# Value products by 64x64 quarters and 32-row tiles, and the second batch's attention turned by VectorE and moved, in a pooled-attention and sine-MLP kernel

## The chip, the cores and the metric

One core of one Trainium2 chip. The metric is device time in microseconds (us), of single executions; smaller is better. A result says "ratio" for the mean time of one kernel's fast runs over the mean time of the kernel before in the same rounds on the same chip, so it is not quite the ratio of the medians that stand beside it. In profile lines PE is TensorE (PEld its weight loads), DVE VectorE, ACT ScalarE, POOL GpSimd, and SPq and ACTq are the DMA issues of SyncE and ScalarE. The granted clock is the share of the full TensorE clock that the throttle let through; "half clock" means stretches where that share is 0.5. A call of the value products leaves two records in a trace (16 for a batch's eight).

## The reference

```python
# q, k, v: (8, 8, 576, 64) float32; w_in (512, 2048), w_out (2048, 512), alpha (2048)
k_p = k.reshape(B, H, 72, 8, D).mean(axis=3)          # 576 keys pooled to 72
v_p = v.reshape(B, H, 72, 8, D).mean(axis=3)
scores = scale * q @ k_p.T                            # (576 x 72) per head
attn = softmax(scores)
x = (attn @ v_p).transpose(0, 2, 1, 3).reshape(4608, 512)
h = x @ w_in
s = np.sin(alpha * h)
out = (h + s * s / (alpha + 1e-9)) @ w_out
```

## The kernel before

TensorE computes both large products with a seven-product scheme: L580 is one line of the hidden product (records of 128x128 against 256 columns), L874 the output product. A batch's attention is spread over the 28 slots of the hidden product of the batch before; a slot is eight L580 records, 1.76 us. Each slot first runs what the slot before left over (`left0` to `left6`: evictions, sines, squares, sums), then the extras that `carry` gives it, then its product. So every engine's order is the program's order.

For a batch from the third on, softmax runs with queries on partitions; VectorE turns the result in 32x32 blocks into a scratch tile `tr`, and twelve DMAs on SyncE's queue move the blocks of each 32-row group onto the right partitions of `aT`. Then 16 records of value products follow, and 16 small ones for the last 64 queries.

```python
def turn(i):
    n = rows[i]
    if i == 0:
        self.tr = self.new_tr().rearrange("p (c h t i) -> p c h t i", c=3, h=H, i=32)
    nc.vector.transpose(out=self.tr[:n, :, :, i, :].rearrange("p c h i -> p h c i"),        # L347
                        in_=ex[:n, i].rearrange("p h (c i) -> p h c i", i=32))

def move(part):
    for a in (2 * part, 2 * part + 1):
        w = 160 if a < 2 else 128
        for c in range(3):
            m = min(32, Sp - 32 * c)
            flat = lambda x: x.rearrange("k h t i -> k h (t i)")[:, :, 0:w]
            nc.sync.dma_start(out=flat(aT[0][32 * c:32 * c + m, a]),                        # L356
                              in_=flat(self.tr[32 * a:32 * a + m, c]))

def values(hp):
    vp = self.vp[b]
    ps = ... else self.abank([P, 4 * P])              # one of three banks in turn
    for e in range(2):
        h = 2 * hp + e
        x = ... aT[0][:, :, h, 0:4, :] ...
        nc.tensor.matmul(ps[64 * e:64 * e + 64, :], vp[:, h, :], x, start=True, stop=True)  # L382
    to_x(ps.rearrange("p (t j) -> p j t", t=4), hp, 0, 512)     # ScalarE evicts, L371

def turn_q(self, b, part):        # the next-but-one batch's q, the same way, through the same scratch
    if part == 0:
        self.tr = self.new_tr()
    # ... part 0, 1: nc.vector.transpose (L162); part 2, 3: sixteen moves (L169)

# carry(u), batches from the third on (cut)
at((12, 12, 13, 14, 14)[i], A.turn, i)
at(14, A.move, 0)
at(15, A.move, 1)
for hp in range(4):
    at((0, 1, 3, 4)[hp], self.load_kv, "v", b, hp)
    if b < last:
        at((12, 13, 14, 17)[hp], self.load_kv, "k", b + 1, hp)   # L109; GpSimd sums them, L114
    at(24, A.values, hp)
at(24, A.values_rest)                                            # L392
at(26, self.att[b + 1].k_t)                                      # TensorE turns the next keys, L194
# turn_q of batch u + 2 at slots 21 to 24
```

The second batch is different: TensorE turns its q (L205) and its attention (L263) itself, ScalarE and VectorE evict, and nothing is moved.

## Time and profile before

| | before |
|---|---|
| median of the first three runs | 952.11 us (950.91 to 952.22) |
| span of the profiled run | 942.5 us, mean granted clock 0.995 |
| TensorE stops over 0.15 us in that span | 16.5 us, 15.5 of them before 95 us |
| first score product of batch three | 111.1 us |
| from there, block to block | 57.5, 58.0, 57.5, 57.5, 57.7 us |
| last block's start to the end | 543.3 us |

How to read it: I use the first score product of each batch as a mile post, because from the third batch on all blocks do the same.

### The profile page before, as it was taken

To read this page: it belongs to the slowest core of one execution; us is meant where nothing else is said; L and a number is where in the kernel's file an instruction comes from. 1 tells how busy PE (TensorE), PEld (TensorE's weight loads), DVE (VectorE), ACT (ScalarE), POOL (GpSimd) and SP (SyncE) were. 2 spreads that over 40 slices of the span, in tenths; PEclk is the share of its full clock that TensorE was granted. 3 is DMA by queue.
4 is the path that set the end of the run, shared out by engine and by line. 5 is a ranking of instruction groups with operands and counts; after the bars stand their busy time and mean duration, and the time that the engine had idled before them with its cause. 6 is when DMAs were issued, how large, how long until landed. Compare 5 with 4: busy or idle time off the path is not lost.

```text
span 942.5 us, 17456 instructions
## 1 busy us (share of the span) xinstructions
PE 920.3 (98%) x6853; PEld 820.5 (87%) x6853; DVE 686.6 (73%) x1025; ACT 441.0 (47%) x1005; POOL 200.4 (21%) x220
## 2 busy tenths in 40 slices
PE   7898999999999999999999999999999999999997
PEld 5576787887878878787888899999999999999997
DVE  6477584766748677485356889988979888979795
ACT  4647576585766758677696651211111111111111
POOL 4337264452634536250000000000000000000000
PEclk9989999999999999999999999999999999999999
DMA  9375456666476663744624545353434444343501
GB/s 249 91 229 154 122 190 154 213 153 201 155 195 190 169 196 97 191 150 135 233 90 136 194 140 146 107 163 90 147 106 129 124 122 131 112 141 90 162 14 38
DMA packets 139841, 137.82 MB, mean 146 GB/s; under 512 B 49088, under 2 KB 108240, under 8 KB 139760
## 3 DMA queue, kind: packets, MB, share of 16 engines
q1 hardware_dynamic: 138688, 135.53, 49.5%
q10 hardware_dynamic: 1072, 1.19, 0.4%
q8 instruction: 54, 0.88, 0.4%
q14 instruction: 27, 0.22, 0.1%
HBM read 74.46 MB, written 47.19 MB: 129 GB/s over the span
## 4 chain that ended last, share of the span: by engine, by line
PE 89%; DVE 3%; DMA 2%; ACT 1%; SPq 1%; POOL 1%; issue 1%; DVEq 0%; ACTq 0%; POOLq 0%
PE PS L580 42%; PE PS L874 40%; PE PS L382 3%; PE PS L224 2%; DMA g_bridge<-h 1%; SPq L356 1%; DMA home<-in_k_dram 1%; ACT s L593 1%; DVE h L559 1%; DMA a<-in_moe_w_in_dram 0%; DVE as L446 0%; DVE tr L347 0%; DVE sm L253 0%; POOL home L121 0%; PE PS L339 0%
## 5 line engine op out<-in xcount | busy, mean ns | idle before, releaser
L580 PE MATMUL PS<-home,a 128*128 128x256 f32 x1152 | 268.2, 384 | 5.5 <-DVE h L559 4.9
L580 PEld LDWEIGHTS PS<-home,a 128*128 128x128 f32 x1152 | 215.9, 191 | 40.0 <-DVE h L559 7.2
L580 PE MATMUL PS<-home,as 128*128 128x256 f32 x864 | 202.4, 382 | 0.3 <-ACT PS L606 0.2
L580 PEld LDWEIGHTS PS<-home,as 128*128 128x128 f32 x864 | 161.3, 190 | 25.1 <-ACT PS L606 3.1
L114 POOL TENSOR_TENSOR kvin<-kvin 72x512 f32<-72x512 f32 x112 | 120.0, 1072 | 159.2 <-DMA kvin<-in_v_dram 103.8
L874 PE MATMUL PS<-s,wb 128*128 128x144 f32 x896 | 119.4, 286 | 0.4 <-ACT PS L987 0.4
L874 PEld LDWEIGHTS PS<-s,wb 128*128 128x128 f32 x896 | 113.7, 190 | 0.7 <-ACT PS L987 0.6
L593 ACT ACTIVATE s<-s,c 128x256 f32<-128x256 f32 (+1 forms) x216 | 110.0, 572 | 0.0
L586 ACT ACTIVATE s<-h,al 128x256 f32<-128x256 f32 x144 | 65.3, 501 | 83.1 <-DVE h L559 83.1
L559 DVE TENSOR_TENSOR h<-PS,p 128x512 f32<-128x512 f32 x72 | 49.2, 683 | 61.2 <-ACT s L593 26.0
L987 ACT COPY PS<-PS 128x144 f32<-128x144 f32 x56 | 14.7, 263 | 145.7 <-PE PS L874 144.3
L586 ACT ACTIVATE s<-PS,al 128x256 f32<-128x256 f32 x144 | 60.0, 467 | 34.9 <-PE PS L580 19.2
L874 PE MATMUL PS<-r,wb 128*128 128x144 f32 x512 | 73.2, 286 | 0.0
L874 PE MATMUL PS<-s,a 128*128 128x144 f32 x512 | 73.2, 286 | 0.0
L874 PEld LDWEIGHTS PS<-r,wb 128*128 128x128 f32 x512 | 67.1, 190 | 0.1
L874 PEld LDWEIGHTS PS<-s,a 128*128 128x128 f32 x512 | 67.1, 190 | 0.0
L647 DVE TENSOR_TENSOR h<-PS,s 128x512 f32<-128x512 f32 x36 | 24.6, 684 | 49.1 <-ACT s L593 48.4
L1006 ACT COPY PS<-PS 128x144 f32<-128x144 f32 x56 | 14.7, 263 | 88.5 <-PE PS L874 88.5
L874 PE MATMUL PS<-s,we 128*128 128x144 f32 x384 | 54.9, 286 | 0.0
L874 PE MATMUL PS<-x,wb 128*128 128x144 f32 x384 | 54.9, 286 | 0.0
L246 POOL TENSOR_TENSOR ex<-ex,sm 128x576 f32<-128x576 f32 (+1 forms) x36 | 40.4, 1147 | 53.2 <-ACT PS L618 21.5
L874 PEld LDWEIGHTS PS<-s,we 128*128 128x128 f32 x384 | 50.4, 190 | 0.1
(146 smaller groups left out, 1218.5 us busy)
## 6 DMA issues: line engine op xcount, KB each, us to landing
g_bridge<-h SPq DMA_DIRECT2D x72, 512.0 KB
r<-g_bridge SPq DMA_DIRECT2D x31, 1152.0 KB
out_dram<-o SPq DMA_DIRECT2D x128, 72.0 KB
kvin<-in_k_dram SPq DMA_DIRECT2D x28, 288.0 KB
kvin<-in_v_dram SPq DMA_DIRECT2D x28, 288.0 KB
q<-in_q_dram SPq DMA_DIRECT2D x7, 1024.0 KB
a<-in_moe_w_in_dram SPq DMA_DIRECT2D x16, 256.0 KB
q<-tr SPq DMA_DIRECT2D x48, 80.0 KB
```

The lines of the kernel that those rows point to most:

```text
L114: (eng or nc.gpsimd).tensor_tensor(out=o, in0=t[:, :, 0:w], in1=t[:, :, w:2 * w], op=OP.add)
L224: nc.tensor.matmul(ps[e][r:r + q.shape[-1], hp, :], q[s], k, start=True, stop=True)
L246: eng.tensor_tensor(out=E(n, i, 0, H), in0=E(n, i, 0, H), in1=sm[:n].unsqueeze(2).to_broadcast([n, H, Sp]), op=OP.mult)
L382: nc.tensor.matmul(ps[64 * e:64 * e + 64, :], vp[:, h, :], x, start=True, stop=True)
L559: add = lambda o, x, y: nc.vector.tensor_tensor(out=o, in0=x, in1=y, op=OP.add)
L580: nc.tensor.matmul(ps[:, jj, :], self.A[p][:, kk, f * P:(f + 1) * P], x[:, kk, :], start=(start and jj == 0 and kk == 0), stop=(kk == 1), ...
L586: nc.scalar.activation(out=G.s[:, i, jj, j, :], in_=src[:, jj], func=AF.Sin, scale=self.al[:, f:f + 1])
L593: nc.scalar.activation(out=x, in_=x, func=AF.Square, scale=self.c[:, f:f + 1])
L647: add = lambda o, x, y: self.nc.vector.tensor_tensor(out=o, in0=x, in1=y, op=OP.add)
L874: nc.tensor.matmul(out, W[:, J // 2, J % 2, :], A[:, J, :], start=(start and J == 0), stop=(J == self.NJ - 1), skip_group_check=True)
L987: nc.scalar.copy(out=x1[:, 0, :], in_=x0[:, 1, :])
L1006: nc.scalar.copy(out=x1[:, 1, :], in_=x1[:, 0, :])
```

## The change

The intent: the value products of 72 keys run in two lanes of 72x64 only. Cut into 64 keys and 8 keys, the 64-key part runs in four 64x64 quarters, and the last eight keys of four heads are put together in one 32-row tile (masked to its heads), so that four of them run side by side. Besides, the second batch is turned by VectorE and moved by DMA like the others, which takes those turnings off TensorE.

```diff
-            aT.append(self.ap.tile([Sp, 4, H, 5, 32], F32, name="aT"))
+            self.aM = self.ap.tile([P, 4, 4, 5, 32], F32, name="aM")     # 64 keys of two heads, one above the other
+            self.aR = self.ap.tile([P, 4, 5, 32], F32, name="aR")        # last 8 keys of four heads, four copies of 32 rows
         def move(part):
-            for a in (2 * part, 2 * part + 1):
-                for c in range(3): ...                                   # 12 moves
+            def heads(a):
+                for s in range(2):
+                    for c in range(2):
+                        r = 64 * s + 32 * c
+                        nc.sync.dma_start(out=flat(self.aM[r:r + 32, a], a), in_=flat(tr[32 * a:32 * a + 32, c, s], a))
+            if part == 0:
+                for a in range(4):
+                    for s in range(2):
+                        nc.sync.dma_start(out=flat(self.aR[32 * s:32 * s + 32, a], a), in_=flat(z[32 * a:32 * a + 32, s], a))
+                heads(0)
+            else:
+                heads(1)
+                for a in range(0, 4, 2):                                 # copies of the rest onto the other rows
+                    x = self.aR[:, a:a + 2, 0:4].rearrange("p a t i -> p a (t i)")
+                    nc.sync.dma_start(out=x[64:], in_=x[:64])
+                heads(2)
+                heads(3)                                                 # 26 moves in all
-        def values(hp): ...
+        def values(hps, banks):
+            for o, (main, _) in zip(ps, parts):
+                for e, (w, x) in enumerate(main):                        # 64x64 quarters, L451
+                    nc.tensor.matmul(o[64 * e:64 * e + 64], w, x, start=True, stop=False, skip_group_check=True)
+            for o, (_, (w, x)) in zip(ps, parts):                        # 32-row tiles, L453
+                nc.tensor.matmul(o, w.rearrange("p e d -> p (e d)"), x, start=False, stop=True, skip_group_check=True)
+            for hp, o in zip(hps, ps):
+                to_x(...)
# carry, steady batches
-            at(15, A.move, 1)
+            at(14, A.move, 1)
-                    at((12, 13, 14, 17)[hp], self.load_kv, "k", b + 1, hp)
-                at(24, A.values, hp)
-            at(24, A.values_rest)
+                    at((12, 13, 15, 18)[i], self.load_k, b + 1, i)
+            at(25, lambda: A.values((0, 2, 1, 3), A.free_banks()))
+            at(26, lambda: A.values_rest((5, (self.turn + 1) % 5)))
# ... second batch: pairs_q, q_t and a_t go; turn_q(1) at slot 2, turn at 17 to 19, move at 19 and 20, values at 25
# ... first batch: laid out for quarters; second weight block and second batch's keys loaded earlier
```

## The prediction

> **What bounds the kernel now.** I read the page's first lines, then the chain that ended last, then TensorE's groups kept apart by shape, and last the timeline of one steady attention batch. The page and its chain:
>
> ```profile
> PE 920.3 (98%) x6853; PEld 820.5 (87%) x6853; DVE 686.6 (73%) x1025; ACT 441.0 (47%) x1005; POOL 200.4 (21%) x220
> PE 89%; DVE 3%; DMA 2%; ACT 1%; SPq 1%; POOL 1%; issue 1%; DVEq 0%; ACTq 0%; POOLq 0%
> ```
>
> TensorE is busy 98% and carries 89% of the chain, so matmul time removed is time gained, provided no wait takes its place. Only about 15 us of TensorE are idle, nearly all before 95 us (window table: 6.43 us in 40 to 50). The longest stop there:
>
> ```profile
> 47.56 0.83 DVE L446 TENSOR_TENSOR as<-a,a 128x512 f32<-128x512 f32 x1 [6.35 <-DMA a<-in_moe_w_in_dram]
> 49.05 3.45 PE L580 MATMUL PS<-home,a 128*128 128x256 f32 x8 [3.80 <-DVE h L559]
> ```
>
> VectorE waits 6.35 us for a weight block queued late, TensorE waits for VectorE. What the change touches on TensorE:
>
> ```profile
> L382 PE MATMUL PS<-aT,vp 72*64 72x512 f32 x128 | 29.7, 600 | 0.6 <-DMA aT<-tr 0.5
> L224 PE MATMUL PS<-kblk,q 64*64 64x72 f32 x912 | 21.2, 229 | 0.0
> L392 PE MATMUL PS<-aT,vp 72*64 72x64 f32 x128 | 5.2, 222 | 0.0
> L263 PE MATMUL PS<-ident,ex 128*72 128x128 f32 x32 | 4.2, 274 | 1.9 <-ACT aT L268 1.9
> L205 PE MATMUL PS<-ident,q 128*128 128x128 f32 x16 | 2.6, 283 | 2.6 <-ACT aT L266 2.6
> ```
>
> The value products (L382, L392) are 35 us over eight batches. L263 and L205 are turnings on TensorE, mostly of the second batch. Now a steady batch: chain, DMA queue and VectorE:
>
> ```profile
> 239.39 31.60 PE PS L580 x144
> 270.99 3.58 PE PS L382 x16
> 274.57 0.46 PE PS L392 x16
> ```
>
> ```profile
> 257.93 3.87 SPq L356 DMA_DIRECT2D aT<-tr  x6
> 261.91 0.60 SPq L109 DMA_DIRECT2D kvin<-in_k_dram  x1
> 262.56 4.15 SPq L356 DMA_DIRECT2D aT<-tr  x6
> ```
>
> ```profile
> 270.31 3.02 DVE L162 STREAM_TRANSPOSE tr<-q 128x1024 f32<-128x1024 f32 x4 [4.91 <-DMA g_bridge<-h]
> 273.26 0.64 DVE L647 TENSOR_TENSOR h<-PS,s 128x512 f32<-128x512 f32 x1
> 273.84 1.20 DVE L647 TENSOR_TENSOR h<-h,s 128x1024 f32<-128x1024 f32 x1
> ```
>
> This is the point of the case. Twelve moves of the turned attention matrix (L356) are issued back to back, 8.0 us for twelve, 0.67 us each with gaps. The semaphores show the first landing 2.5 us after its issue, the last at 270.14. Value products start at 270.99: **the slack is 0.8 us**. VectorE's next turning of q (L162) reuses the same scratch tile, so it waits for the same landing, and everything behind it on VectorE waits too.
>
> **What the Trainium skill says.** "TensorEngine Tiling (Array Packing)", Key Properties: different tiles load and multiply in parallel, and changing the tiling mode drains TensorE. The trace agrees: 32 records of L224 in four quarters take 0.66 us; a slot of eight L580 records takes 1.92 us after such a switch, against 31.60/18 = 1.76 in a row, so a return costs 0.17 us. "DMA: Bandwidth & Descriptors", Rules for kernel authors: many small transfers should be merged, under 64 KB one pays mostly overhead. The trace agrees: 40 KB and 160 KB moves both hold the queue 0.53 to 0.74 us. "TensorE: Matmul & The Clock Gate", What's actually happening: a free-running window of about 3.4 us without work halves the clock. The trace agrees: after the 3.80 us stop above, eight records took 3.45 us instead of 1.9. The same page, under the array's architecture, calls VectorE and ScalarE strict FIFO; L647 behind L162 shows it.
>
> **The change part by part.**
>
> Value products, batches 2 to 8. Before: 16 records of 512 columns in two lanes, 3.58 us. Eight rows of 439 ns (two passes of 512 columns at the 2.33 columns/ns of 256x2/219 ns) make 3.51, so the two lanes are full. After: main part, 16 records in four lanes, 4 x 0.44 = 1.76 us; the last eight keys, 8 records in four lanes, 2 x 0.44 = 0.88. Together 2.64, a saving of 0.9. Against it one more switch between tilings (0.1 to 0.2), 24 records instead of 16 in the rest (0.46 becomes about 0.55), and one more return because the rest moves to the next slot (0.17). **Net about -0.3 to -0.5 us a batch, some -3 us in all.** That is the intent, and it is small.
>
> First two batches on TensorE: q turnings (L205) -3.1, attention turnings (L263) -5.2, value sums in two column lanes (3.9 + 1.2 become about 2.2) -2.9, fewer turnings at the start -0.7, values -1: about -13 us of TensorE work before 110 us. The weight block is also queued earlier, which removes most of the 6.4 us wait. VectorE gains work in the same stretch: turning q 3.0, turning attention 5 x 0.8 = 4.0, the rest's normalisation 1.8, less copies -3.9: about +5 us where it was already 98% busy (70 to 80 us).
>
> The moves. The order of the built program shows 26 DMAs a batch in place of 12: 8 of 32 rows into the new rest tile, 16 of 32 rows into the main tile, 2 copies of the rest onto the other rows. Row count, not size, seems to set their issue (32 rows: 0.53 to 0.61 whatever the bytes). So 26 x 0.63 = 16.4 us instead of 8.0, plus about 2.2 to the last landing: 18.6 after the first issue instead of 12.2. They still start when the fifth attention turning is done (about 0.4 earlier, since 512+64 columns turn a little faster than 768). Value products move one slot (1.76 us) later. In the batch above: last landing 257.5 + 18.6 = 276.1; the slot comes at 270.99 + 1.76 = 272.7. **TensorE stops about 3.4 us in every batch from the third on.** I take this as the main effect.
>
> What follows the landing, batches 3 to 7. L162 starts only then, 3.0 us, L647 1.84: to 281.0. ScalarE's sine and square (L586, L593, 1.74 us) need L647 to free their tile, and the values' evictions now stand behind them, because they moved a slot: first eviction done about 283.4. The rest of the values reuses that bank: it would be ready at 276.2 + 2.85 + 1.92 = 281.0, so it waits 2.4 us more. Also two loads of the next keys stand behind the 26 moves; those keys are summed near 283, no worse. Batch time: the next hidden block starts at 283.6 + 0.9 + 3.7 = 288.2 instead of 282.5, **+5.8 us**. Stops of 3.4 and 2.4 us can trip the half clock, perhaps +0.6 on average. Five such batches: +32. The last batch has no q to turn: +3.5.
>
> Second batch. TensorE reaches its values early, but the fifth turning is emitted at slot 19 and the values at slot 25, about 11 us later, while the moves need 19. Walking the engines' orders with the durations above, I get the fifth turning done near 79 us, landing near 98, the next block at 110 against 109.4 before: the 13 us saved turn into one stop of over 10 us. About +1, with a half clock after it.
>
> Sum: +32 +3.5 +1 = +36 us at face value, 988. I take off some 10 us for what such a sum tends to overrate (a move that issues faster, overlaps that I put in series): **978 us**.
>
> **The rivals.** (a) TensorE stays the bound and the moves stay hidden. Speaking for it: 98% busy, and whoever shifted values and key loads by a slot had some delay in view. Then -13, -3 and up to -4 of the weight wait: 932 to 940, on the edge of 2%. Against it: 0.8 us of slack and 14 more issues of a very regular 0.6 us. (b) VectorE becomes the bound in the first 110 us, moves hidden elsewhere: the gain shrinks to about 5 to 10 us, 942 to 947. Its 98% there speaks for it, 73% over all against more. (c) Moves issue in 0.4 us, as 128-row loads do in the trace (0.37 to 0.39): 26 x 0.45 = 11.7, landing about 3.5 us later than before, a stop of some 1 us; the chain through L162 is nearly gone: 945 to 955. Against it: 32-row moves never took under 0.53. (d) My main line without its second half (evictions not held up): 3.4 x 6 = +20, clock +3, second batch 0, values -2: 970 to 975.
>
> **Range and chances.** Main line and (d) hold about 0.75, (c) 0.12, (a) and (b) together 0.13. The range 953 to 1000 covers (d), the main line and its overshoot, and touches (c). Faster than 933 needs (a) at its best: 0.05. Within 2% (933 to 971): (b), (c), and the low end of (d): 0.24. Slower: 0.71.
>
> **What would show each step right or wrong.** Right: the DMA queue shows 26 move issues in a row of about 16 us in each batch; values wait for a DMA into the new tiles, 3 to 4 us each; L162's successor waits about 10 us instead of 5 for its tile; ScalarE's evictions follow its sine; half-clock stretches appear. TensorE's busy time falls by some 12 to 18 us while the span grows. The new value products show about 2.6 us a batch instead of 3.6. Wrong: moves at 0.45 us or less, or no wait ahead of the values; then I have overrated the queue. If values take 3.5 us or more, the lanes did not overlap. If the second batch's end moves before 105 us, my walk there was too pessimistic.

## The result, and the profile after

The changed kernel takes 1000.4 us in the median of four runs (994.17 to 1006.93); the kernel before, on the same chip, 951.51. The ratio is 1.0528, 95% interval 1.0449 to 1.0607: slower. That lies 0.4 us outside the predicted range of 953 to 1000, far less than the 12.8 us by which the four runs scatter, so on which side of the edge it fell was chance.

The profiled execution of the kernel after is the slowest of its four (span 1005.2 us), that of the kernel before a quick one (942.5), so the two traces differ by 62.7 us where the medians differ by 49. The page of the kernel after, busy times and the chain that ended last:

```profile
PE 945.3 (94%) x6946; PEld 834.4 (83%) x6946; DVE 692.6 (69%) x1072; ACT 434.3 (43%) x1002; POOL 183.1 (18%) x209
PE 67%; SPq 12%; DVE 7%; DMA 6%; ACT 3%; issue 2%; POOL 1%; DVEq 0%; ACTq 0%
```

TensorE carried 89% of the chain and now carries 67%; SyncE's queue went from 1% to 12%. TensorE's busy time did not fall but rose by 25 us. From 170 to 460 us its mean granted clock is 0.94, where it was 1.00. An estimate from the two traces, busy time less half of what ran at half clock (the time before the first full clock counted as half): 916 us before and 911 after, so at full clock the work fell by some 6 us.

TensorE's groups of the kernel after, by shape (records, busy us and mean ns, then idle time ahead of them and what ended it):

```profile
L451 PE MATMUL PS<-aM,vm 64*64 64x512 f32 x128 | 27.9, 786 | 23.7 <-DMA aM<-tr 23.7
L453 PE MATMUL PS<-aR,vz 32*128 32x512 f32 x64 | 10.2, 640 | 0.0
...
L476 PE MATMUL PS<-aR,vz 32*128 32x64 f32 x64 | 5.5, 308 | 0.0
L473 PE MATMUL PS<-aM,vm 64*64 64x64 f32 x128 | 4.0, 242 | 12.6 <-ACT home L423 9.8 <-ACT aM L371 2.8
```

The value products, which waited 0.6 us in all, now wait 23.7 for the moves, and their rest, which waited for nothing, 12.6 for evictions. These groups mix stretches of full and of half clock; a clean figure for the products comes from an experiment below.

One steady batch of the kernel after, in order of time (start, length, engine and line, records; in brackets the idle time before it and what ended it):

```profile
162.49 1.35 SPq L406 DMA_DIRECT2D aR<-aR  x2
...
163.88 5.19 SPq L395 DMA_DIRECT2D aM<-tr  x8
...
169.17 0.49 SPq L95 DMA_DIRECT2D kvin<-in_k_dram  x1
...
169.49 2.98 PE L451 MATMUL PS<-aM,vm 64*64 64x512 f32 x16 [1.78 <-DMA aM<-tr]
...
170.57 3.01 DVE L180 STREAM_TRANSPOSE tr<-q 128x1024 f32<-128x1024 f32 x4 [10.18 <-DMA aM<-tr]
...
175.40 0.84 ACT L672 ACTIVATE s<-PS,al 128x256 f32<-128x256 f32 x2 [8.26 <-DVE h L733]
...
177.63 0.46 PE L473 MATMUL PS<-aM,vm 64*64 64x64 f32 x16 [2.17 <-ACT home L423]
...
178.96 2.06 POOL L104 TENSOR_TENSOR kvin<-kvin 72x512 f32<-72x512 f32 x2 [1.10 <-DMA kvin<-in_k_dram]
...
181.61 0.38 PE L212 MATMUL PS<-ident,kp 72*128 72x72 f32 x1 [1.48 <-POOL kp L104]
```

The last eight moves are issued up to 169.07. The value products start at 169.49 and wait once more among themselves. VectorE's turning of q (L180) waits 10 us for its scratch tile; ScalarE's sine waits for VectorE's sums; the rest of the values waits for evictions behind the sine. And the next batch's third and fourth key loads stand in the queue behind all 26 moves. The fourth is issued at 170.76 and lands at 178.89, GpSimd sums it until 181.5, and the last turning of the keys (L212) waits for that. (In the kernel before, the fourth load stood behind the moves as well, but was summed before TensorE came to it.)

The second batch of the kernel after, the first moves and the value products:

```profile
89.44 5.03 SPq L400 DMA_DIRECT2D aR<-tr  x8
...
107.27 4.03 PE L451 MATMUL PS<-aM,vm 64*64 64x512 f32 x16 [10.40 <-DMA aM<-tr]
```

The fifth turning ends at 89.4, 26 moves follow in 17.2 us, and TensorE stops for 10.4 us. In the six batches after it the 26 issues take 16.7 to 17.4 us, and in all seven the last landing comes 1.4 to 1.6 us after the last issue ends.

The mile posts of the two traces:

| | before | after |
|---|---|---|
| first score product of batch three | 111.1 | 121.7 |
| blocks | 57.5, 58.0, 57.5, 57.5, 57.7 | 67.2, 65.4, 67.3, 67.7, 68.2 |
| last block's start to the end | 543.3 | 547.6 |
| half clock before 900 us | 6.8 us | 61.4 us |

So the five steady blocks cost 47.8 us of the 62.7, the stretch before them 10.6, the last block 4.3. A caution on the 10.6: the clock becomes full for the first time at 7.7 us in this trace of before and at 25.2 in this one of after, and such a late start is chance: the same code of the first two batches reached the post at 111.1 (start at 7.7) or, with hardly changed first batches in three experiments, at 113.6 (start at 6.9), 116.7 and 118.3 (starts at 24.9) before, and after at 118.2 (start at 6.8) as well as 121.0 and 121.7 (starts at 23.5 and 25.2). Like against like, the second batch costs some 3 to 7 us; the 7 holds only against the one trace of before that had no half clock again between 10 and 21 us. Where the queue was relieved, the second batch cost nothing that can be seen: e2 reached the post at 110.3 and e4 at 111.4 (starts at 6.8 and 7.3).

### The profile page after: what moved, and what is told of

The parts are those of the page before. It is cut to its first block, busy times and chain, and to the rows that moved or that the text cites. A ratio compares the mean times of both kernels' runs of the same rounds, so it can differ in the third digit from the quotient of the medians.

```text
span 1005.2 us, 17842 instructions
## 1 busy us (share of the span) xinstructions
PE 945.3 (94%) x6946; PEld 834.4 (83%) x6946; DVE 692.6 (69%) x1072; ACT 434.3 (43%) x1002; POOL 183.1 (18%) x209
## 4 chain that ended last, share of the span: by engine, by line
PE 67%; SPq 12%; DVE 7%; DMA 6%; ACT 3%; issue 2%; POOL 1%; DVEq 0%; ACTq 0%
PE PS L964 38%; PE PS L666 24%; SPq L395 6%; DMA kvin<-in_k_dram 4%; SPq L400 3%; PE PS L231 2%; DVE tr L380 2%; DMA g_bridge<-h 2%; DVE h L733 1%; POOL kvin L104 1%; ACT s L679 1%; SPq L406 1%; DVE h L645 1%; DVE sm L260 1%; SPq L740 1%
## 5 line engine op out<-in xcount | busy, mean ns | idle before, releaser
L666 PE MATMUL PS<-home,a 128*128 128x256 f32 x1152 | 272.8, 388 | 0.1
L666 PEld LDWEIGHTS PS<-home,a 128*128 128x128 f32 x1152 | 219.6, 194 | 39.9 <-issue 5.3
L666 PE MATMUL PS<-home,as 128*128 128x256 f32 x864 | 210.4, 394 | 3.3 <-ACT PS L692 3.1
L666 PEld LDWEIGHTS PS<-home,as 128*128 128x128 f32 x864 | 168.5, 198 | 28.4 <-ACT PS L692 3.5
L104 POOL TENSOR_TENSOR kvin<-kvin 72x512 f32<-72x512 f32 (+5 forms) x105 | 103.8, 989 | 235.8 <-DMA kvin<-in_v_dram 122.1
L672 ACT ACTIVATE s<-h,al 128x256 f32<-128x256 f32 x144 | 65.8, 510 | 71.3 <-DVE h L645 71.2
L180 DVE STREAM_TRANSPOSE tr<-q 128x1024 f32<-128x1024 f32 (+1 forms) x28 | 21.2, 809 | 71.2 <-DMA aM<-tr 71.2
```

What stands on the lines that cost most here:

```text
L104: self.nc.gpsimd.tensor_tensor(out=t[..., 0:w] if w > D else out, in0=t[..., 0:w], in1=t[..., w:2 * w], op=OP.add)
L180: nc.vector.transpose(out=out, in_=x)
L666: nc.tensor.matmul(ps[:, jj, :], self.A[p][:, kk, f * P:(f + 1) * P], x[:, kk, :], start=(start and jj == 0 and kk == 0), stop=(kk == 1), ...
L672: nc.scalar.activation(out=G.s[:, i, jj, j, :], in_=src[:, jj], func=AF.Sin, scale=self.al[:, f:f + 1])
```

## The experiments

Lines in an experiment's kernel are numbered a little differently where code was added.

### e1: the queue alone, in the kernel before

```diff
         def move(part):
+            if part == 0 and b > 1:
+                for n in range(14):            # nobody reads them
+                    r, c = 32 * (n % 4), 64 * (n // 4)
+                    nc.sync.dma_start(out=self.extra[r:r + 32, c:c + 64], in_=...tr[r:r + 32, 0, 0]...[:, 0:64])
# move 1 at slot 14, key loads at 12, 13, 15, 18, values at 25, rest at 26, as in the kernel after
```

> The kernel before, with its own value products and its second batch untouched, but from the third batch on the DMA queue of the kernel after: 14 small moves of 32 rows (256 bytes a row, into a tile that nobody reads) ahead of the 12 real ones, key loads and value slots as in the kernel after. Result stays correct. Theory (26 issues in a row on one queue make the values late): six batches each lose 7 to 9 us, TensorE waits 4 to 7 us for the last move ahead of the values; about 990 to 1005 us against 951. Rival 1 (the quarters, the 32-row tiles and their tiling switches cost the time): nothing changes, 951 to 960. Rival 2 (the reordered first two batches cost it): nothing changes either.

Measured: 993.9 us (990.33 to 998.79), ratio 1.0459 [1.0422, 1.0495], correct. The steady blocks take 65.8, 66.1, 64.8, 65.1, 68.1. One batch of it, value products:

```profile
231.71 2.80 PE L386 MATMUL PS<-aT,vp 72*64 72x512 f32 x12 [1.34 <-DMA aT<-tr]
...
238.85 1.98 PE L386 MATMUL PS<-aT,vp 72*64 72x512 f32 x4 [4.34 <-ACT home L375]
```

Fourteen transfers that nobody reads turn the kernel before into nearly the kernel after. The total is as the theory had it; its parts are not. The wait for the landing is 1.3 us here and less in the other batches, not 4 to 7, and the larger stop (4.3 us) comes behind it: the fourth pair of products needs a bank (there are three), its eviction stands behind ScalarE's sine, and that behind VectorE's sums and its turning of q. Both rivals, which left this run unchanged, fall as the main cause. The later slots came in together with the dummies here; that the slots alone cost nothing is shown by e2, which has them too.

### e2: the kernel after without the ten moves of the last eight keys

```diff
             self.aR = self.ap.tile([P, 4, 5, 32], F32, name="aR")
+            if b:
+                nc.gpsimd.memset(self.aR[:], 0.0)     # wrong result on purpose
-                for a in range(4): ...                # 8 moves into aR
-                for a in range(0, 4, 2): ...          # 2 copies
```

> The kernel after without the ten moves of the last eight keys (the rest tile is zeroed by GpSimd instead, so the result is wrong on purpose; same TensorE work). Sixteen issues remain, 10 us, landing 2 us later. Theory: the last move lands about 12.5 us after the first issue, before the value slot; the stops ahead of the values go to under 0.5 us from the third batch on, the second batch lands 6 us earlier; about 940 to 955 us. Rival (quarters and 32-row tiles themselves are slow): stays above 985. Rival (the first batches): only some 6 to 10 us back, 990.

Measured: 949.23 us, ratio 0.9994 [0.9949, 1.0039]; the result is wrong, as intended. Steady blocks 58.4, 57.8, 58.3, 58.1, 59.0. One batch:

```profile
272.32 1.95 PE L447 MATMUL PS<-aM,vm 64*64 64x512 f32 x16
274.19 1.14 PE L449 MATMUL PS<-aR,vz 32*128 32x512 f32 x8
...
277.19 0.46 PE L469 MATMUL PS<-aM,vm 64*64 64x64 f32 x16
...
277.58 0.66 PE L472 MATMUL PS<-aR,vz 32*128 32x64 f32 x8
```

All the TensorE work of the change is still there and 50 us are gone: the new products are not slow. It also gives their clean price, from start to start of records: quarters 1.88, 32-row tiles 1.07, rest 0.39 + 0.59, together 3.93 us. In the kernel before the same is 3.48 + 0.56 = 4.04. One more return to the large tiling (0.17, from 1.92 against 1.76) makes it even. **The intended gain of the quarters is nothing**, even with no wait ahead of them. The block is still 0.7 us longer than before on average; the turning of the keys, 1.20 us instead of 0.26 here and 0.56 to 1.93 over the five batches, more than covers that.

### e3: a scratch tile of its own for q

```diff
         if part == 0:
-            self.tr = self.new_tr()
+            self.trq = self.ap.tile([P, 4 * self.NP * 160], F32, name="trq")[:]
```

> The kernel after, with a scratch tile of its own for the turning of q, so that VectorE need not wait for the landing of the moves. Theory (the landing holds up VectorE, its sums hold up ScalarE's sine, and that holds up the evictions of the values): the first stop, ahead of the values, stays at about 2.5 us a batch; the second one, ahead of the rest of the values (2.2 us), goes; 2 to 3 us a batch in five batches, a little more with less half clock: 980 to 990 us. Rival (the evictions are late by themselves, whatever VectorE does): within 4 us of the kernel after.

Measured: 1006.33 us, ratio 1.0561 [1.0517, 1.0604]: a miss. The batch that answers to the one shown of the kernel after:

```profile
177.94 0.46 PE L473 MATMUL PS<-aM,vm 64*64 64x64 f32 x16
...
180.91 0.38 PE L212 MATMUL PS<-ident,kp 72*128 72x72 f32 x1 [1.09 <-POOL kp L104]
```

The wait ahead of the rest is gone, as predicted, and the block is as long as before: from the first value product to the last key turning 12.16 us here, 12.12 there. Two things took its place. The waits for GpSimd's key sums grew (9.5 us in the whole run instead of 5.1), though not in this batch; and half clock came earlier and longer: here it ran from 170.3 to 177.1 us, under the values, and over the five steady blocks it made 47.8 us instead of 37.5, while all of TensorE's stops there fell from 26.7 us to 21.3. VectorE was free early, yet the third and fourth key loads still stood behind the moves.

### e6 and e9: the key loads ahead of the moves, with and without the own scratch tile

```diff
-                    at((12, 13, 15, 18)[i], self.load_k, b + 1, i)
+                    at((11, 12, 13, 14)[i], self.fetch_k, b + 1, i)   # the DMA, ahead of the moves
+                    at((12, 13, 15, 18)[i], self.pool_k, b + 1, i)    # GpSimd's sums, as before
```

> The kernel after with the own scratch tile for q (which alone gave nothing: the wait ahead of the rest went, and a wait of equal size for the next keys came in its place) and with the last two key loads queued ahead of the moves instead of behind them. Theory (two late chains side by side, each hidden behind the other): both second stops go, only the one ahead of the values stays (1.8 to 2.5 us and 0.8 inside); 4 us a batch less idle and less half clock; 965 to 982 us. Rival (something else is late too, VectorE's sums or the evictions): 995 or more. Rival (the moves start later behind the key loads): the first stop grows by 1 to 2 us, 985 to 995.

> The kernel after with the last two key loads queued ahead of the moves, and nothing else (the scratch tile stays shared). With the own scratch tile alone and with both on record, this fills the square. Theory (the late keys end the batch, and the wait ahead of the rest of the values lies hidden before them): the key wait of TensorE goes, the wait ahead of the rest stays at about 2 us; 1 to 2.5 us a batch, 990 to 998 us. Rival (both are needed together): as the kernel after, 1000 or more. Rival (the scratch tile never mattered): all of the gain of the pair, 991 or less.

Measured: e6 991.2 us, ratio 1.0452 [1.0403, 1.0500]; e9, without the own tile, 995.0 us, ratio 1.0499 [1.0475, 1.0522]. The five steady blocks add up to 335.8 us in the kernel after, 335.3 in e3, 325.5 in e9 and 322.3 in e6. So in the traces early keys are worth some 2 us a batch, the scratch tile at most 0.6. The times do not separate them: the interval of e9 lies within that of the kernel after (1.0449 to 1.0607) and overlaps that of e6, and the trace of the kernel after is of its slowest run, that of e9 of its quickest. e6 missed what I expected of it (965 to 982). One batch of e9:

```profile
301.41 4.23 PE L460 MATMUL PS<-aM,vm 64*64 64x512 f32 x16 [3.44 <-DMA aM<-tr]
...
310.34 0.46 PE L482 MATMUL PS<-aM,vm 64*64 64x64 f32 x16
```

Two things ate the rest. The moves now start behind the key loads, and the stop ahead of the values grew from 1.8 us to 3.4 in this batch. And the rest of the values did not wait although the scratch tile is shared, against what I expected: after that stop TensorE ran at half clock (the eight products between took 2.82 us, not 1.99) and came to the rest when the evictions were done. I had put the evictions and the half clock in a row; here they run side by side.

### e4: two queues

```diff
-                heads(2)
-                heads(3)
+            elif part > 1:
+                heads(part, nc.scalar)      # issued from ScalarE
+            at(16, A.move, 2)
+            at(17, A.move, 3)
```

> The kernel after, with the last 8 of the 26 moves issued two and three slots later from ScalarE's queue instead of SyncE's; same bytes, same TensorE and VectorE work, result correct. Theory (the time lies in issuing one after the other): SyncE issues 18 in 11.3 us, all land about 13.5 us after the first issue, just before the value slot; stops under 1 us; 950 to 965 us. Rival (the transfers themselves, shared DMA engines, take the time): the landing does not move, 995 or more. Rival (ScalarE, busy with 5 us of issues, becomes the late one): stops move to the evictions, 975 to 990.

Measured: 963.02 us, ratio 1.0132 [1.0096, 1.0169], correct. Steady blocks 59.6 to 61.8. One batch:

```profile
206.86 1.99 PE L666 MATMUL PS<-home,a 128*128 128x256 f32 x8 [1.31 <-ACT PS L704]
206.90 2.70 ACTq L395 DMA_DIRECT2D aM<-tr  x4
207.61 5.45 SPq L395 DMA_DIRECT2D aM<-tr  x8
...
219.15 1.95 PE L451 MATMUL PS<-aM,vm 64*64 64x512 f32 x16
```

The same 26 transfers with the same bytes, eight of them issued elsewhere, and from the third batch on the value products wait for nothing (in the second batch 3.9 us, instead of 10.4). So the time was in issuing one after the other and not in the transfers. "DMA: Bandwidth & Descriptors" of the Trainium skill, under Issuing engines are not separate DMA queues, says that several issuing engines save only the time it takes to initiate a DMA, "usually small relative to the DMA itself". The trace agrees with the first half; the second does not hold for such a row of moves: issuing took about 17 us for 26 moves, landing 1.5 more, and taking eight of the issues to another queue brought the ratio from 1.0528 to 1.0132. What is left over before is partly ScalarE: its issues hold up an eviction that TensorE needs (1.31 us above).

### e7: filling the stops

```diff
+            at(25, fill, 8, 5)                            # eight 128x128 matmuls into the next product's bank
             at(25, lambda: A.values((0, 2, 1, 3), A.free_banks()))
+            at(26, lambda: fill(8, (self.turn + 1) % 5))
             at(26, lambda: A.values_rest((5, (self.turn + 1) % 5)))
```

> The kernel after with 8 idle-filling matmuls of 128x128 into the bank that the next product overwrites, ahead of the values and again ahead of their rest, in batches three to eight (some 2 us of TensorE work each, where it stops 1.8 to 2.4 us). Nothing arrives sooner; only the idle time is filled. Theory (the half clock follows the stops): the half-clock stretches of 6.8 us from 170 us on go or shrink to one of 3.4, their cost being half their length, 2 to 3 us a batch: 980 to 990 us. Rival (half clock has another cause): the same stretches stay and the fillers cost up to 1 us a batch: 1000 to 1010.

Measured: 998.65 us, ratio 1.0523 [1.0458, 1.0588]. The clock did as expected, the time did not. The same window of both kernels, busy us of TensorE, weight loads, VectorE, ScalarE, GpSimd, then the mean granted clock; first the kernel after, then e7:

```profile
170.00:460.00 290.00, 264.73 (x1868) 208.00 (x1865) 163.94 (x294) 166.80 (x365) 104.52 (x115) 0.94 0.56 159
```

```profile
170.00:460.00 290.00, 278.05 (x2171) 226.53 (x2164) 170.94 (x314) 173.23 (x379) 109.52 (x124) 0.99 0.56 161
```

From 181 us on there is no half clock, and the blocks shrink by 2.0 us on average (66.4, 63.8, 65.0, 65.6, 65.0); these are the traces of the quickest run of e7 and the slowest of the kernel after. But a fill takes 1.95 us and some wait stays behind it, 1.9 to 3.1 us in all where the stop was 0.9 to 2.4, and over all runs nothing is gained that I could tell from the scatter of the kernel after. So the half clock follows the stops and is no second cause; its price, about 2 us a batch, I take from the traces and not from the times, which do not show it.

### e5: only the second batch

The kernel before with VectorE turning the second batch, twelve moves, the early loads, and the slots of the kernel after for the second batch up to its moves; its value products and all later batches keep the slots of before.

```diff
-                at((21, 22, 22, 23, 23)[i], A.a_t, i, 0)  # and pairs_q, q_t, a_t(i, 1)
+            for part in range(4):
+                at(2, self.turn_q, 1, part)
+                at((17, 17, 18, 19, 19)[i], A.turn, i)
+            at(19, A.move, 0)
+            at(20, A.move, 1)
```

> The kernel before with only the second part of the change: second batch turned by VectorE and moved (12 moves, as the others), weight block and keys loaded early, schedule of the first blocks as in the kernel after; value products in two lanes as before. Result correct. Theory (the loss is the number of moves, not who turns the second batch): the steady blocks stay at 57.5 us; in the second batch TensorE stops 2 to 4 us for the landing; some 13 us of TensorE work saved, most of it lost again to stops: 942 to 953 us. Rival (turning the second batch by VectorE is what costs): block two ends 8 to 10 us later than before, 960 or more.

Measured: 955.51 us, ratio 1.0067 [1.0031, 1.0103], correct. Steady blocks 57.5 to 58.1. The post of batch three is at 118.3 (before 111.1, both with an early clock, but with half clock again from 13.2 to 20.0 here and not there), with a stop of 7.7 us ahead of the values. Both expectations have a part: the steady loss is not from here, but this part alone costs up to 7 us in the trace and 6 in the times, though it takes work off TensorE, and though only 12 moves are made. The fifth turning ends at 87.8.

### e10, e11, e13: what holds up the second batch

Each adds one step to the one before: e10 lets VectorE do the divisions, e11 queues the third batch's keys behind the moves, e13 puts VectorE's sums of the fourth weight block behind the turnings.

```diff
-            divide(i, sm, nc.gpsimd)
+            divide(i, sm, nc.vector if b == 1 else nc.gpsimd)                          # e10
-                at((17, 18, 19, 20)[i], self.load_kv, "k", 2, i)
+                at((20, 21, 22, 23)[i], self.load_kv, "k", 2, i)                       # e11
-                at((4, 10, 14)[J - 1], self.combine_w_in, J, 0)
-                at((6, 12, 15)[J - 1], self.combine_w_in, J, 1)
+                at((4, 10, 20)[J - 1], self.combine_w_in, J, 0)                        # e13
+                at((6, 12, 21)[J - 1], self.combine_w_in, J, 1)
```

> The kernel before with only its second batch turned by VectorE (955.5 us), and there the division of the attention rows done by VectorE instead of GpSimd, which is busy summing values at 66 to 80 us. Theory (VectorE's turnings waited for GpSimd's divisions, and those for the summing of values): the fifth turning ends near 84 instead of 88 us, TensorE's stop of 7.7 us ahead of the values falls to about 4; 949 to 953 us. Rival (VectorE itself is full there): no change or slower, 955 or more.

> As the run before this one, with the key loads of the third batch queued behind the 12 moves of the second instead of between them. Theory: the landing comes 1 to 3 us earlier still, the stop ahead of the values shrinks to 1 to 3 us; 946 to 951 us, level with or just under the kernel before. Rival (those keys are then late at the end of the batch): a stop at the turning of the keys, 950 to 955.

> As the run with VectorE's divisions and the keys behind the moves (953.3 us), with VectorE's four sums of the fourth weight block (0.7 to 1.75 us each, 4.6 in all) moved from ahead of the attention's normalisation to behind its turnings; the block is first used later still, so the result stays correct. Theory (in the second batch VectorE's own queue is the bound: what stands ahead of the turnings delays them, and TensorE with them): the fifth turning and the sums that TensorE waits for come 4 to 5 us earlier, the 3.4 us stop near 85 us and the 2.3 us stop ahead of the values shrink by that, less half clock; 946 to 950 us. Rival (the bound there is ScalarE's exponentials with their table loads, or the DMA queue): same stops, 952 to 955.

Measured: 953.63 us, ratio 1.0059 [1.0037, 1.0080]; 953.34 us, 1.0054 [1.0032, 1.0076]; 951.4 us, 1.0036 [1.0007, 1.0066]. All three miss on the slow side. e13's trace says why taking work out of VectorE's queue did so little:

```profile
72.98 0.76 DVE L253 TENSOR_REDUCE sm<-ex 128x8 f32<-128x584 f32 x1 [3.94 <-ACT ex L241]
```

```profile
86.23 5.29 PE L580 MATMUL PS<-home,a 128*128 128x256 f32 x16 [5.56 <-DVE h L559]
...
98.79 2.84 PE L382 MATMUL PS<-aT,vp 72*64 72x512 f32 x8 [3.81 <-DMA aT<-tr]
```

VectorE, with 4.6 us less ahead of it, waits 3.9 us for ScalarE's exponential; in e5 it waited 3.1 us for GpSimd's division; TensorE waits for VectorE's sums behind the turnings, and then for the moves. The fifth turning ended at 87.8 in e5 and 87.9 in e13. So in these traces three engines each hold the next up, and relieving one brings the next into view. That VectorE alone is the bound there, as I had it, is refuted. Which order of the three would free the block is left open.

### e8 and e14: the early weight block alone

```diff
         self.load_q(1)
+        self.load_w_in_part(1)
-            at(2, self.load_w_in_part, 1)
```

> The kernel before with one line moved: the second block of the first weights is queued behind the second q instead of behind the keys of the second batch (the change has this too). Theory: VectorE's 6.35 us wait for that block near 47 us goes, TensorE's 3.8 us stop behind it goes or halves, with the half-clock stretch of 6.8 us after it: 944 to 949 us against 951. Rival (the keys that now stand behind it become the late ones): no change, 949 to 953.

> The kernel before with the second weight block queued earlier, once more, with more rounds: the first time 0.9983 of the kernel before, interval 0.9946 to 1.0020. If the 1 to 2 us that the trace shows less of TensorE's stops are real, 946 to 949 us and an interval under 1; if not, level.

Measured: 948.54 us, ratio 0.9983 [0.9946, 1.0020], and with more rounds 948.21 us, 1.0002 [0.9975, 1.0029]. Level. VectorE's long wait for that block goes, and with it TensorE's stop of 3.8 us; TensorE stops instead for 1.4 to 2.9 us at the turning of the keys, which now stand behind the block. (Its stop of 2.6 us at the turning of q is there with and without the edit.)

### e12: the kernel after with the remedies

Moves on two queues (ScalarE's one slot later, behind its copies), own scratch tile, third key load ahead of the moves, divisions of the second batch on VectorE.

> The kernel after with all remedies at once: eight of the 26 moves from ScalarE's queue one slot later than in the run with two queues (behind ScalarE's copies), own scratch tile for q, the third key load ahead of the moves, divisions of the second batch on VectorE. Result correct. Theory: steady blocks of 58.2 to 58.8 us as in the run without rest moves, the second batch's stop 4 us instead of 10; 948 to 956 us. So the change with every wait taken away would be level with the kernel before, as quarters and rest save nothing net (2.95 + 0.98 + a return of 0.2 against 3.48 + 0.56 us a batch in the run without rest moves). Rival (ScalarE's issues still hold up its copies): 957 to 965.

Measured: 958.46 us, ratio 1.0111 [1.0090, 1.0132], correct. Steady blocks 58.7, 58.4, 58.5, 59.3, 58.8: there the theory held but for one block, and the value products wait for no move. But the time is in the range of the rival: ScalarE's issues still hold up its copies (TensorE waits 3.6 us for them over the five blocks). And the second block ends at 119.7, where I had expected a gain. e4, without the other remedies, was there at 111.4, and its interval overlaps that of e12, so in the times they added nothing that can be told. Up to 3.4 us of the 8 can be clock (6.9 us of half clock at 14.2 to 21.1 us in e12 alone). The divisions on VectorE may be another: the fifth turning ended at 88.6 here, and at 85.6 in e7, which leaves them on GpSimd and has the same late half clock; one trace each, so this is not shown. So the whole change, with its queue relieved, is still 1% behind the kernel before: 1 us a block, where the products save nothing and ScalarE's issues cause small stops, and the second batch. No version that I ran beats the kernel before.

## Why the prediction was wrong, point by point

The mechanism was right: 26 issues of a regular 0.63 us, a landing after the value slot, a chain over VectorE and ScalarE, half clock. The direction and most of the size follow from it. The step that failed is the sum, in four of its terms: the next keys, "summed near 283, no worse", cost 1.65 us a batch; the half clock, "perhaps +0.6", cost 2.2; the second batch, "about +1", cost 3 to 7; and some 10 us were taken off for overlaps that did not come. That put the time 22 us over the estimate. One steady block, from the traces (start to start of TensorE's records, 254.4 to 321.7 us of the kernel after against 226.6 to 284.1 before):

| term, us a batch | predicted | measured |
|---|---|---|
| stop ahead of and among the values | 3.4 | 1.8 + 1.7 |
| stop ahead of the rest | 2.4 | 2.3 |
| value products, rest, tiling returns | -0.3 to -0.5 | 0.0 to 0.1 |
| half clock | 0.6 | 2.2 |
| turning of the next keys | 0 ("no worse") | 1.65 |
| sum | 6.4 (block 5.8, clock 0.6) | 9.7 (blocks: 67.3 - 57.5 = 9.8) |

The lines behind it, first of the kernel before, then of the kernel after:

```profile
278.53 0.42 PE L194 MATMUL PS<-ident,kp 72*128 72x72 f32 x4
```

```profile
302.18 1.07 PE L451 MATMUL PS<-aM,vm 64*64 64x512 f32 x4 [1.84 <-DMA aM<-tr]
303.87 1.93 PE L451 MATMUL PS<-aM,vm 64*64 64x512 f32 x12 [0.61 <-DMA aM<-tr]
...
311.11 0.46 PE L473 MATMUL PS<-aM,vm 64*64 64x64 f32 x16 [2.30 <-ACT home L423]
...
313.96 0.38 PE L212 MATMUL PS<-ident,kp 72*128 72x72 f32 x1 [1.11 <-POOL kp L104]
```

The predicted terms as listed add up to 6.0; the walk's own times have the two stops at 3.5 and 2.6, which makes up most of the rest. The measured ones are of the slowest of the four runs. The median lies 6.5 us lower, and which term is smaller there is not known.

- **26 moves, about 16 us.** Right: 16.7 to 17.4 us, and 18.2 to 18.8 from the first issue to the last landing, where 18.6 was predicted. e1, e2 and e4 show that it is their number in one queue, not their bytes and not the products.
- **The stop of 3.4 us.** Right in size, in two pieces: 1.84 us ahead of the first record, and 3.55 us for records that take 1.88 when nothing waits (e2). In the two steady batches before it the same came to 2.8 and 3.0.
- **The chain through L162, L647 and the sine to the evictions.** Right as a chain: e3 removed its wait. But as a cost it stood beside others, not in a row: with the own tile alone the block was as long as before.
- **"Those keys are summed near 283, no worse".** Failed. The last two key loads wait behind 26 issues, the fourth took 7.5 us from issue to landing in the batch of the table, and TensorE waits for its sum. In the traces e9 got 2 us a batch back with the keys alone.
- **"Perhaps +0.6 on average" for the half clock.** Undersized: 61 us of half clock in the trace, some 2 us a batch (e7's trace). The scatter of the kernel after over 13 us it does not explain: its four runs have nearly the same mean granted clock (0.969, 0.969, 0.971, 0.969). That mean leaves out the time before the first full clock, which came anywhere from 5.6 to 25.2 us in these traces; whether that is the cause is open.
- **The second batch, "about +1".** Failed: the walk put the fifth turning near 79 us, it ended at 89.4. Some 4 to 6 us of these 10 are the late clock of that trace: with nearly the same code up to there it ended at 84.3, 83.5 and 85.6 in e2, e4 and e7, whose clock was early, and at 88.1 to 88.8 in e3, e6 and e9, whose clock was late. For the rest, I had counted VectorE's work and not its waits for GpSimd and ScalarE. The stretch to the post cost 3 to 7 us instead of 1; the "stop of over 10 us" was 10.4.
- **Some 10 us taken off the sum** for overlaps. No measurement supported that; the sum at face value, 988, was nearer, and what I had left out was larger than what I had overrated.
- **The last batch, +3.5**: 4.3.
- **Products.** Quarters 1.76 predicted, 1.88 measured; 32-row tiles 0.88 and 1.07; the rest 0.55 and 0.98, the larger miss: it is eight records of 32 rows more at 64 columns, and they cost 0.59 us by themselves.
- **TensorE's busy time was to fall by 12 to 18 us.** It rose by 25, since a record takes twice as long at half clock (L666 0.43 us from start to start instead of 0.22); at full clock it would have fallen by some 6 (the estimate above). A busy figure is no measure of work where the clock changes.
- **Slips in the readings and sums.** "32 rows: 0.53 to 0.61 whatever the bytes": the batch that was read has 0.56 to 0.64 for 32 rows, and 0.67 to 0.74 for its smallest moves, of 8 rows, so the row count alone does not set the issue time. In rival (c), 11.7 + 2.2 us is 1.7 later than the 12.2 of before, not 3.5, and with the values a slot later it would have meant no stop. The tail of "about 2.2" after the last issue was 1.4 to 1.6 for the new moves; the larger ones of the kernel before took 3.0 to 3.9.

## What to carry to other kernels

Before a change to a layout is judged by what it saves on the array, count the transfers it needs in one queue and multiply by the measured time of one issue; here 14 more issues of 0.63 us outweighed the products whatever these saved. Look for what stands in that queue behind the new transfers, not only for who waits for the transfers themselves. And when two waits end at nearly the same time, taking away one can only uncover the other, or let half clock fill the gap (e3, and in part the second batch), so a null result of one says little until both have been taken away.

## What the Trainium skill lacked or had wrong

- "DMA: Bandwidth & Descriptors", Issuing engines are not separate DMA queues: that the time to initiate is usually small beside the DMA does not hold for rows of small moves within SBUF: 26 issues take 16.7 to 17.4 us, the last lands 1.4 to 1.6 us after them, and eight of them issued from ScalarE took the ratio from 1.0528 to 1.0132 (e4).
- No page that I found gives the issue time by shape: moves of 32 rows hold SyncE's queue for a median of 0.59 to 0.61 us with 256 to 5120 bytes a row (e1 and before), the eleven loads of q with 128 rows for a median of 0.38, and key loads of 72 rows for 0.85.
- "TensorE: Matmul & The Clock Gate", HAM oscillation — how this bites in real kernels: its rule of no idle gaps over about 3.4 us is too lenient. Stops of 1.8 to 2.4 us were enough here. I cut each of the sixteen traces into stretches of 3.413 us, so that the changes of clock fall on their edges, and added up TensorE's idle time in each stretch of full clock. Each of the 52 stretches with more than 2.0 us of it was followed by half clock; between 1.1 and 2.0 us, 30 were and 61 were not; below that, none.
- "TensorEngine Tiling (Array Packing)", Key Properties: it names the drain at a change of tiling but gives no figure; a return to the 128x128 tiling costs about 0.17 us here after the score products and after the 32-row tiles (1.92 to 1.93 against 1.76 for eight records), but only 0.05 after the 72x64 value products of the kernel before (3.56 against 3.51 for sixteen).
